# Every second softmax tile masked by ScalarE and GpSimd, with sb in three places

## The chip, the core and the metric

The kernel runs on one core of a Trainium2 chip. The metric is the device time of one execution in microseconds (us), the median of several runs. The engines are called PE (TensorE matmuls; PEld are its weight loads), DVE (VectorE), ACT (ScalarE), POOL (GpSimd) and SP (SyncE, which issues the DMAs).

## The reference

Attention in which each query keeps its 32 best scores, and behind it an expert layer with a product of two projections:

```
scores = scale * np.matmul(q, k.transpose(0, 1, 3, 2))      # q, k, v: (4, 8, 576, 64)
kth = np.partition(scores, -top_k, axis=-1)[..., -top_k:-top_k + 1]      # top_k = 32
scores = np.where(scores >= kth, scores, -1000000000.0)
scores = scores - np.max(scores, axis=-1, keepdims=True)
attn = np.exp(scores)
attn = attn / (np.sum(attn, axis=-1, keepdims=True) + 1e-09)
x = np.matmul(attn, v)                     # then as (2304 tokens, 512)
out = ((x @ w_a) * (x @ w_b)) @ w_out      # w_a, w_b: (512, 1536), w_out: (1536, 512)
```

## The kernel before

**Tiles and chunks.** The 2304 tokens are eight chunks: each of the four batches has one of 256 tokens and one of 320. Attention goes through 144 tiles in order. A tile is 64 queries of two heads against all 576 keys, so a matrix of 128 x 576; four tiles make a head pair of a chunk of 256 tokens, five one of 320. Tiles 0 to 15 are chunk 0, 16 to 35 chunk 1, 36 to 51 chunk 2, 52 to 71 chunk 3, and so on to 143.

**One tile.** `scores` has PE write the scores s to PSUM (L422; two places). `topk` has ScalarE copy them to sb in SBUF (two places), and VectorE finds the 32 largest in two columns' minima and maxima with MAX8 and MATCH_REPLACE8 (L442 to L452). The 32nd, `tb[:, g, 31:32]`, is the threshold. The tiles are taken in groups of two (GRP), so an even tile and the odd one behind it share the tiles mx and top, and behind the odd one GpSimd subtracts a 128x2 piece (L456, short). `softmax` then masks and exponentiates in one of two ways:
- P (the letter is that of the changed kernel): ScalarE makes r = relu(threshold - s) from PSUM (L470), PE subtracts a huge multiple of it from s by two bf16 matmuls with `nident` (L475), and ScalarE takes the exponential of s from PSUM with its sum (L477). s stays taken until then. Of the scores only half is copied to sb (L435).
- V: all of s is copied to sb (L433), ScalarE takes the exponential of sb (L464), and VectorE multiplies it by (sb >= threshold) and sums (L466).

Tiles 0 to 34 are P. From 35 to 109 the even ones are V and the odd ones P; from 110 on all are V. Behind either way come a small ScalarE step, VectorE's reciprocal (L480) and the scaling of p, by GpSimd (L484), or from tile 50 on by ScalarE in even tiles (L482). `transpose` turns p on PE (L497) and ScalarE copies it (L502). At the last tile of a head pair, `av` has PE multiply it with v (L525). When a chunk has all its pairs, its experts can run.

**Experts.** `up` makes a tile of the two projections from 12 matmuls each (L555 to L557, high and low parts), ScalarE or VectorE takes the product (L564, L569; L572 and L573 in the first two chunks), ScalarE writes gh and GpSimd the rest gl (L574, L575). `down` multiplies all of gh and gl with w_out (L585 to L587).

**What sets the order.** Nothing in the program runs in the order in which it is written. `Plan` lists all operations with an engine, a cost, a key and the buffers they need. It then goes through them with an event queue: an engine that is free takes the ready operation with the lowest key whose buffers have a place. Attention has keys from -1000 on, transpositions and weightings 0 to 143, experts 1000 and more, so experts fill what attention leaves of PE. Where PE has nothing to do and no product waits, Plan puts a filler matmul (L291, `mm<-still,nident`). The list that comes out is each engine's program, and each engine runs its own list strictly in order. In Plan's costs a masking pass of VectorE (`port=True`) takes 0.4 us longer when GpSimd is busy at its start.

```
plan.filler = (lambda: buf([128, 512], FT, "mm", 2, psum), FILL_N / 2353,
               lambda b: mm(b[:, 0:FILL_N], nident, still, start=True, stop=True))
ATTENTION, URGENT, EXPERTS = -1000, -1500, 1000
```

Of the kernel before, what the change touches and what calls it, by code (L numbers as in the profile page):

```python
# [8 lines left out]
FT = mybir.dt.float32  # L9
# [5 lines left out]
AF = mybir.ActivationFunctionType  # L15
OP = mybir.AluOpType
AX = mybir.AxisListType

HUGE = float(2.0 ** 94)
# [4 lines left out]
GRP = 2  # L24


VECTOR_MASK = (35, 110)
SCALAR_SCALE = 50
POOL_PRODUCT = 2
CONV_FIRST = 14  # L30
# [220 lines left out]
def attn_moe(ctx: ExitStack, tc, qT, kT, v, wa, wb, wo, out):  # L251
# [5 lines left out]
    nc = tc.nc  # L257
    B, NP, _, S = qT.shape
    NJ = wa.shape[0]
    HS = S // 2  # L260
# [18 lines left out]
        tiles += [dict(c=c, p=p, pair=c * NP + p, off=64 * s, s=s, n=n) for s in range(n // 64)]  # L279
    NT = len(tiles)  # L280

    def vector_mask(i):
        return i >= VECTOR_MASK[0] and i % 2 == 0 or i >= VECTOR_MASK[1]


    plan = Plan()
    key = [0.0]
    still = const.tile([128, FILL_N], BF, name="still")
# [4 lines left out]
    def buf(shape, dtype, tag, bufs, pool=work):  # L293
        return Buf(pool, shape, dtype, tag, bufs)

    def act(n, fn, r, w, ps=False, ptr=0, k=None):
        plan.op("ACT", n / 1200 + (0.085 if ps else 0.11) + 0.075 * ptr + 0.035 * (n == 1), key[0] if k is None else k, fn, r, w)

    def dve(n, fn, r, w, cost=None, k=None, port=False):
        plan.op("DVE", cost or (n + 76) / 960, key[0] if k is None else k, fn, r, w, port=port)  # L300

    def pool(n, fn, r, w, cost=None):
        plan.op("POOL", cost or 0.2 + n / 480, key[0], fn, r, w)

    def pe(cols, fn, r, w, rows=1.0, num=0, k=None):
        plan.op("PE", cols / 2300 + 0.009 * num, key[0] if k is None else k, fn, r, w, rows=rows)
# [119 lines left out]
    def topk(i, s):  # L426

        alone = vector_mask(i)  # L430
        sb = buf([128, 2, HS], FT, "sb", 2)
        if alone:
            act(S, lambda: nc.scalar.activation(sb.ap, s[:, :, 0:HS], AF.Copy), [s], [sb], ps=True)  # L433
        else:
            act(HS, lambda: nc.scalar.activation(sb[:, 1], s[:, 1, 0:HS], AF.Copy), [s], [sb], ps=True)  # L435
        g = i % GRP
        if g == 0:
            tops.append((buf([128, GRP, HS + 8], FT, "mx", 2), buf([128, GRP, 32], FT, "top", 2)))
        mx, tb = tops[-1]
        mn, t8, bias = buf([128, HS], FT, "mn", 1), buf([128, 8], FT, "t8", 2), buf([128, 1], FT, "bias", 3)  # L440

        dve(HS, lambda: vec.tensor_tensor(mn.ap, s[:, 0, 0:HS], sb[:, 1], OP.min), [s, sb], [mn])  # L442
        dve(HS, lambda: vec.max(mx[:, g, HS:HS + 8], mn.ap), [mn], [(mx, g, 1)])
        dve(HS, lambda: vec.tensor_tensor(mx[:, g, 0:HS], s[:, 0, 0:HS], sb[:, 1], OP.max), [s, sb], [(mx, g, 0)])
        tk = [t8] + [(tb, g, r) for r in range(1, 4)]

        def eight(r):
            return tb[:, g, 8 * r:8 * r + 8] if r else t8.ap
        for r in range(4):
            dve(HS + 8, lambda r=r: vec.max(eight(r), mx[:, g]), [(mx, g, 0), (mx, g, 1)], [tk[r]], 0.393)  # L450
            if r < 3:
                dve(HS + 8, lambda r=r: vec.match_replace(mx[:, g], eight(r), mx[:, g], LOW), [tk[r]], [(mx, g, 0), (mx, g, 1)], 0.453)  # L452
            if r == 0:
                act(1, lambda: nc.scalar.activation(bias.ap, t8[:, 0:1], AF.Copy, scale=-0.125), [t8], [bias], k=URGENT)
        if g == GRP - 1:
            pool(g, lambda: nc.gpsimd.tensor_tensor(short[:, i - g:i + 1], tb[:, :, 31], mx[:, :, HS + 7], OP.subtract),  # L456
                 [(mx, x, y) for x in range(GRP) for y in (0, 1)] + [(tb, x, 3) for x in range(GRP)], [("short", i)])
        return bias, (tb, g, tk[3]), sb

    def softmax(i, s, found):  # L460
        bias, (tb, g, tok), sb = found
        pt, sm = buf([128, 2, HS], FT, "p", 3), buf([128, 2], FT, "sm", 3)
        if vector_mask(i):
            act(S, lambda: nc.scalar.activation(pt.ap, sb.ap, AF.Exp, bias=bias.ap, scale=0.125),  # L464
                [sb, bias], [pt], ptr=1)
            dve(S, lambda: vec.scalar_tensor_tensor(pt.ap, sb.ap, tb[:, g, 31:32], pt.ap, op0=OP.is_ge, op1=OP.mult,  # L466
                                                    accum_out=sm[:, 0:1]), [sb, tok], [pt, sm], 0.735, port=True)
        else:
            r = buf([128, 2, HS], BF, "r", 2)
            act(S, lambda: nc.scalar.activation(r.ap, s[:, :, 0:HS], AF.Relu, bias=tb[:, g, 31:32], scale=-1.0),  # L470
                [s, tok], [r], ps=True, ptr=1)

            def mask():
                for g in range(2):
                    mm(s[:, g, 0:HS], nident, r[:, g], start=False, stop=True, skip_group_check=True)  # L475
            pe(S, mask, [r], [s])
            act(S, lambda: nc.scalar.activation(pt.ap, s[:, :, 0:HS], AF.Exp, bias=bias.ap, scale=0.125,  # L477
                                                accum_out=sm[:, 0:1]), [s, bias], [pt, sm], ps=True, ptr=2)
        act(1, lambda: nc.scalar.activation(sm[:, 1:2], sm[:, 0:1], AF.Copy, bias=1e-9), [], [sm], k=URGENT)
        dve(1, lambda: vec.reciprocal(sm[:, 1:2], sm[:, 1:2]), [], [sm])  # L480
        if i >= SCALAR_SCALE and i % 2 == 0:
            act(S, lambda: nc.scalar.activation(pt.ap, pt.ap, AF.Copy, scale=sm[:, 1:2]), [sm], [pt], ptr=1)  # L482
        else:
            pool(0, lambda: nc.gpsimd.tensor_scalar(pt.ap, pt.ap, sm[:, 1:2], 1.0, op0=OP.mult, op1=OP.mult), [sm], [pt], 0.81)  # L484
        return pt
# [113 lines left out]
    for i, t in enumerate(tiles):  # L599
        c, pi = t["c"], t["pair"]  # L600
        key[0] = ATTENTION + i
        s = scores(i)
        pt = softmax(i, s, topk(i, s))
        key[0] = i + TURN
        transpose(i, pt)
# [177 lines left out]
```

## Time and profile before

| | |
|---|---|
| median of 3 runs | 899.75 us (899.21 to 903.09) |
| the profiled execution | 903.89 us, of which the span is 902.2 us |
| mean granted TensorE clock in its span | 0.982 |
| busy: PE, PEld, DVE | 834.0 (92%), 663.4 (74%), 747.3 us (83%) |
| busy: ACT, POOL | 566.8 (63%), 321.3 us (36%) |
| chain of work that ended last, by engine | PE 73%, DVE 11%, ACT 5%, POOL 3%, DMA 3% |

An engine's busy time is the union of its instructions' times. Matmuls overlap in a pipeline and their ends are modelled, so what one costs is read from the starts of those around it.

### The profile page before, as it was taken

To read this page: it belongs to the slowest core of one execution; us is meant where nothing else is said; L and a number is where in the kernel's file an instruction comes from. 1 tells how busy PE (TensorE), PEld (TensorE's weight loads), DVE (VectorE), ACT (ScalarE), POOL (GpSimd) and SP (SyncE) were. 2 spreads that over 40 slices of the span, in tenths; PEclk is the share of its full clock that TensorE was granted. 3 is DMA by queue.
4 is the path that set the end of the run, shared out by engine and by line. 5 is a ranking of instruction groups with operands and counts; after the bars stand their busy time and mean duration, and the time that the engine had idled before them with its cause. 6 is when DMAs were issued, how large, how long until landed. Compare 5 with 4: busy or idle time off the path is not lost.

```text
span 902.2 us, 18725 instructions
## 1 busy us (share of the span) xinstructions
PE 834.0 (92%) x6461; PEld 663.4 (74%) x6461; DVE 747.3 (83%) x2310; ACT 566.8 (63%) x1334; POOL 321.3 (36%) x431
## 2 busy tenths in 40 slices
PE   3767779997999999999999999999999999999997
PEld 1433347765768867887787888787878888899997
DVE  4899888999999999999999999999999999960010
ACT  3678667995767776777666676677666665651120
POOL 2677655885335541232213231122212221331120
PEclk8999999998999999999999999999999999999999
DMA  5767754874336741476226662377326732475450
GB/s 192 235 220 237 233 177 154 313 249 149 106 112 210 221 138 57 125 252 228 87 68 217 207 202 80 103 241 240 116 81 213 245 117 77 139 232 172 141 208 28
DMA packets 75430, 153.87 MB, mean 171 GB/s; under 512 B 7232, under 2 KB 46144, under 8 KB 75328
## 3 DMA queue, kind: packets, MB, share of 16 engines
q1 hardware_dynamic: 75328, 152.60, 52.6%
q8 instruction: 53, 0.87, 0.4%
q14 instruction: 49, 0.40, 0.2%
HBM read 135.27 MB, written 17.30 MB: 169 GB/s over the span
## 4 chain that ended last, share of the span: by engine, by line
PE 73%; DVE 11%; ACT 5%; POOL 3%; DMA 3%; issue 3%; SPq 1%; POOLq 0%; ACTq 0%; DVEq 0%
PE mm L555 11%; PE mm L557 10%; PE mm L556 10%; PE s L422 8%; PE tp L497 7%; PE mm L525 7%; PE mm L585 6%; PE mm L587 5%; PE mm L586 5%; DVE mx L452 3%; DVE top L450 2%; PE s L475 2%; DMA wo<-wb 1%; POOL wo L389 1%; DMA gh<-wb 1%
## 5 line engine op out<-in xcount | busy, mean ns | idle before, releaser
L555 PE MATMUL mm<-xh,w 128*128 128x256 f32 (+1 forms) x768 | 241.9, 315 | 1.8 <-DMA w<-wd 1.7
L557 PE MATMUL mm<-xh,w 128*128 128x256 f32 (+1 forms) x768 | 226.8, 295 | 0.0
L556 PE MATMUL mm<-xl,w 128*128 128x256 f32 (+1 forms) x768 | 226.5, 295 | 0.0
L450 DVE MAX8 top<-mx 128x8 f32<-128x296 f32 x432 | 196.1, 459 | 2.9
L555 PEld LDWEIGHTS mm<-xh,w 128*128 128x128 f32 x768 | 144.6, 188 | 30.6 <-issue 27.0
L556 PEld LDWEIGHTS mm<-xl,w 128*128 128x128 f32 x768 | 144.9, 189 | 0.0
L557 PEld LDWEIGHTS mm<-xh,w 128*128 128x128 f32 x768 | 144.2, 188 | 0.0
L502 ACT ACTIVATE pt<-tp 128x640 f32<-128x640 f32 x144 | 101.2, 703 | 66.8 <-PE tp L497 66.2
L575 POOL TENSOR_TENSOR gl<-a,gh 128x256 fp32r<-128x256 f32 (+1 forms) x96 | 78.4, 817 | 175.2 <-ACT gh L574 172.9
L452 DVE MATCH_REPLACE8 mx<-top,mx 128x296 f32<-128x296 f32 x288 | 129.9, 451 | 0.0
L422 PE MATMUL s<-kr,qr 64*64 64x288 f32 x1152 | 107.3, 442 | 17.8 <-ACT p L477 10.7
L585 PE MATMUL mm<-gh,wo 128*128 128x256 f32 (+1 forms) x384 | 122.0, 318 | 0.3 <-ACT b L591 0.2
L484 POOL TENSOR_SCALAR p<-p,sm 128x576 f32<-128x576 f32 x97 | 81.1, 836 | 111.6 <-DVE sm L480 104.4
L497 PE MATMUL tp<-ident,p 128*128 128x128 f32 x720 | 104.8, 276 | 12.7 <-POOL p L484 11.6
L586 PE MATMUL mm<-gl,wo 128*128 128x256 f32 (+1 forms) x384 | 114.2, 297 | 0.4 <-POOL gl L575 0.4
L587 PE MATMUL mm<-gh,wo 128*128 128x256 f32 (+1 forms) x384 | 114.4, 298 | 0.1
L497 PEld LDWEIGHTS tp<-ident,p 128*128 128x128 f32 x720 | 82.7, 141 | 28.8 <-POOL p L484 20.5
L569 DVE SCALAR_TENSOR_TENSOR a<-mm,a 128x256 f32<-128x256 f32 (+1 forms) x72 | 32.8, 455 | 79.2 <-PE mm L557 76.3
L585 PEld LDWEIGHTS mm<-gh,wo 128*128 128x128 f32 x384 | 73.3, 191 | 16.6 <-issue 13.6
L525 PE MATMUL mm<-pt,vr 128*64 128x256 f32 (+1 forms) x640 | 84.7, 411 | 0.8 <-ACT pt L502 0.6
L442 DVE TENSOR_TENSOR mn<-s,sb 128x288 f32<-128x288 f32 x144 | 64.4, 447 | 18.8 <-ACT sb L435 17.7
L586 PEld LDWEIGHTS mm<-gl,wo 128*128 128x128 f32 x384 | 73.4, 191 | 0.6 <-POOL gl L575 0.6
(82 smaller groups left out, 1459.2 us busy)
## 6 DMA issues: line engine op xcount, KB each, us to landing
w<-wd SPq DMA_DIRECT2D x168, 512.0 KB, 4.4
wd<-w SPq DMA_DIRECT2D x24, 512.0 KB, 3.4
kr<-kT SPq DMA_DIRECT2D x64, 144.0 KB, 3.0
vr<-v SPq DMA_DIRECT2D x32, 256.0 KB, 2.9
wo<-wa SPq DMA_DIRECT2D x12, 512.0 KB, 5.2
qr<-qT SPq DMA_DIRECT2D x32, 160.0 KB, 3.2
wo<-wb SPq DMA_DIRECT2D x9, 512.0 KB, 5.7
qr<-qT SPq DMA_DIRECT2D x32, 128.0 KB, 3.0
```

What stands on the lines that cost most here:

```text
L422: mm(s[rows, g, 0:HS], qr[on, h, t["off"]:t["off"] + 64], kr[on, h, :], start=True, stop=True)
L450: dve(HS + 8, lambda r=r: vec.max(eight(r), mx[:, g]), [(mx, g, 0), (mx, g, 1)], [tk[r]], 0.393)
L452: dve(HS + 8, lambda r=r: vec.match_replace(mx[:, g], eight(r), mx[:, g], LOW), [tk[r]], [(mx, g, 0), (mx, g, 1)], 0.453)
L497: nc.tensor.transpose(tp[:, kb, :], pf[:, k0:k0 + 128], ident)
L502: act(640, lambda: nc.scalar.activation(turned[:, :, :, t["off"]:t["off"] + 64], tp.ap.rearrange("p k (h q) -> p k h q", h=2), AF.Copy), [ ...
L525: mm(ps[e, :n], vr[:, kb, e], turned[:, kb, h, :n], start=(kb == 0), stop=(kb == 4))
L555: mm(ps[:, :n], w[:, 0, kb, :], xh[:, kb, :n], start=(kb == 0), stop=False)
L556: mm(ps[:, :n], w[:, 0, kb, :], xl[:, kb, :n], start=False, stop=False)
L557: mm(ps[:, :n], w[:, 1, kb, :], xh[:, kb, :n], start=False, stop=(kb == 3))
L585: mm(ps[:, :n], fin[j][:, 0, ms], gh[:, j, :n], start=(j == 0), stop=False)
L586: mm(ps[:, :n], fin[j][:, 0, ms], gl[:, j, :n], start=False, stop=False)
L587: mm(ps[:, :n], fin[j][:, 1, ms], gh[:, j, :n], start=False, stop=(j == NJ - 1))
```

## The change

The pair of numbers that told V tiles apart becomes a string with a letter for each tile. Tiles 0 to 34 stay P, even tiles from 36 on are V as before, and all odd tiles from 35 on become Q: the 38 from 35 to 109 were P, the 17 from 111 to 143 were V. No tile from 35 on is masked through PE. In a Q tile GpSimd makes threshold x HUGE (far), ScalarE makes relu(far - HUGE x sb) from the copy in SBUF, GpSimd subtracts that from sb (576 columns, two inputs), and ScalarE takes the exponential with its sum. All of s is copied to sb for Q as for V, and sb has three places for two.

```diff
-VECTOR_MASK = (35, 110)
+MASKS = "P" * 35 + "QV" * 55
...
-    def vector_mask(i):
-        return i >= VECTOR_MASK[0] and i % 2 == 0 or i >= VECTOR_MASK[1]
...
-        alone = vector_mask(i)
-        sb = buf([128, 2, HS], FT, "sb", 2)
-        if alone:
+        sb = buf([128, 2, HS], FT, "sb", 3)
+        if MASKS[i] != "P":
             act(S, lambda: nc.scalar.activation(sb.ap, s[:, :, 0:HS], AF.Copy), [s], [sb], ps=True)
...
-        if vector_mask(i):
+        if MASKS[i] == "Q":
+            far = buf([128, 1], FT, "far", 2)
+            pool(1, lambda: nc.gpsimd.tensor_scalar(far.ap, tb[:, g, 31:32], HUGE, None, op0=OP.mult), [tok], [far])
+            act(S, lambda: nc.scalar.activation(pt.ap, sb.ap, AF.Relu, bias=far.ap, scale=-HUGE), [sb, far], [pt], ptr=1)
+            pool(S, lambda: nc.gpsimd.tensor_tensor(pt.ap, sb.ap, pt.ap, OP.subtract), [sb], [pt])
+            act(S, lambda: nc.scalar.activation(pt.ap, pt.ap, AF.Exp, bias=bias.ap, scale=0.125, accum_out=sm[:, 0:1]),
+                [bias], [pt, sm], ptr=2)
+        elif MASKS[i] == "V":
```

Plan makes a new order from this. Up to the end of chunk 0's experts the lists are the same. In the changed kernel line numbers are 4 or 5 lower up to `topk`, and 2 higher from `softmax`'s V branch on.

PE around the weighting of tile 71 (pt and vr), the last of chunk 3, before. Ahead of it end the up products of chunk 2 (xh, xl), behind it begin its down products (gh, gl):

```order
L557 MATMUL mm<-xh,w 128x256
L497 MATMUL tp<-ident,p 128x128 x5
L291 LDWEIGHTS nident
L291 MATMUL mm<-still,nident 128x256
...
L525 MATMUL mm<-pt,vr 64x320 x10
L497 MATMUL tp<-ident,p 128x128 x5
L422 MATMUL s<-kr,qr 64x288 x4
L475 LDWEIGHTS nident
L475 MATMUL s<-r,nident 128x288
...
L585 MATMUL mm<-gh,wo 128x256
```

The same place now:

```order
L499 MATMUL tp<-ident,p 128x128 x5
L557 MATMUL mm<-xh,w 128x256
L558 MATMUL mm<-xl,w 128x256
L559 MATMUL mm<-xh,w 128x256
L527 MATMUL mm<-pt,vr 64x320 x10
L418 MATMUL s<-kr,qr 64x288 x4
L499 MATMUL tp<-ident,p 128x128 x5
L587 MATMUL mm<-gh,wo 128x256
```

Four fillers (one of them is shown) and a mask's two matmuls are gone, and up products stand right ahead of the weighting, where before there were fillers. Of the other fillers from 250 us on, the 9 ahead of tile 35's weighting have become 19, and 7 around the end of chunk 1's up products have become 2.

DVE in chunk 3, where the last two tiles (70 is V, 71 is Q) and the first two of chunk 4 meet, before. top_5831 belongs to tiles 70 and 71, top_6014 to the next two; L466 is the masking pass of a V tile, L450 into top a step of the search, L480 the reciprocal:

```order
L466 SCALAR_TENSOR_TENSOR p_5843,sm_5877<-sb_5750,top_5831,p_5843 128x576
...
L450 MAX t8_5983<-mx_5957 128x8
L450 MAX top_5831<-mx_5782 128x8
L452 MATCH_REPLACE mx_5957<-t8_5983,mx_5957 128x296
...
L480 RECIPROCAL sm_6022<-sm_6022 128x1
```

The same place now; here top_5858 belongs to tiles 70 and 71, and sm_6033 is tile 71's:

```order
L468 SCALAR_TENSOR_TENSOR p_5845,sm_5932<-sb_5709,top_5858,p_5845 128x576
L447 MATCH_REPLACE mx_5791<-top_5858,mx_5791 128x296
...
L445 MAX top_5858<-mx_5791 128x8
L438 MAX mx_5974<-mn_5953 128x8
...
L482 RECIPROCAL sm_6033<-sm_6033 128x1
L445 MAX top_6024<-mx_5974 128x8 x2
L447 MATCH_REPLACE mx_5974<-top_6024,mx_5974 128x296 x2
L445 MAX top_6024<-mx_5974 128x8 x2
L468 SCALAR_TENSOR_TENSOR p_6019,sm_6096<-sb_5876,top_6024,p_6019 128x576
```

Between tile 71's last MAX and its reciprocal stand 8 vector operations before and 12 now (among them three replacements), and 19 now between that MAX and the next masking pass (among them five replacements).

POOL in the same stretch, before (gl is the experts', short the 128x2 piece of a pair, L484 the scaling):

```order
L575 TENSOR_TENSOR gl_5254<-a_5857,gh_5250 128x256
L575 TENSOR_TENSOR gl_5254<-a_5912,gh_5250 128x256
L456 TENSOR_TENSOR short_99<-top_5831,mx_5782 128x2
L575 TENSOR_TENSOR gl_5254<-a_5970,gh_5250 128x256
L484 TENSOR_SCALAR p_6021<-p_6021,sm_6022 128x576
```

Now:

```order
L577 TENSOR_TENSOR gl_5289<-a_5888,gh_5283 128x256
L451 TENSOR_TENSOR short_99<-top_5858,mx_5791 128x2
L460 TENSOR_SCALAR far_5984<-top_5858 128x1
L577 TENSOR_TENSOR gl_5289<-a_5928,gh_5283 128x256
L462 TENSOR_TENSOR p_5993<-sb_5772,p_5993 128x576
L577 TENSOR_TENSOR gl_5289<-a_5986,gh_5283 128x256
L486 TENSOR_SCALAR p_5993<-p_5993,sm_6033 128x576
```

The product far and the subtraction of tile 71 (p_5993) have come between the short piece and the scaling, each next to an expert's gl. In 39 of the 55 Q tiles nothing stands between far and the subtraction; in 4 the memset of vr (L336 now) does, which waits for PE.

## Rows read from the trace of the kernel before

**Rows 1.** Busy by stage: window, length, PE, PEld, DVE, ACT, POOL, clock, DMA.
```profile
250.00:434.00 184.00, 180.01 (x1435) 142.44 (x1433) 173.84 (x573) 130.25 (x319) 64.39 (x96) 1.00 0.54 170
434.00:625.00 191.00, 189.71 (x1520) 152.36 (x1521) 179.57 (x595) 132.09 (x317) 46.44 (x78) 1.00 0.50 156
625.00:802.00 177.00, 176.61 (x1367) 148.56 (x1367) 169.71 (x547) 110.64 (x246) 41.97 (x68) 1.00 0.49 155
802.00:902.20 100.20, 93.77 (x716) 91.28 (x715) 8.10 (x20) 18.85 (x45) 15.08 (x20) 0.99 0.43 144
```

**Rows 2.** What PE waited for, 250 to 802 us: total, times, longest.
```profile
PE tp L497 <- POOL p L484: 3.5, 5, 1.1
PE s L475 <- ACT r L470: 1.1, 2, 0.8
PE s L422 <- ACT p L477: 0.5, 2, 0.3
```

**Rows 3.** The mask's matmuls on PE (L475) in a window, columns as in rows 1.
```profile
250.00:625.00 375.00, 15.85 (x76) 1.00 0.52 162
```

**Rows 4.** Timeline of PE: a mask between two experts (start, duration).
```profile
329.52 0.31 PE L557 MATMUL mm<-xh,w 128*128 128x320 f32 x1
329.67 0.42 PE L475 MATMUL s<-r,nident 128*128 128x288 bf16 x2
329.83 0.40 PE L555 MATMUL mm<-xh,w 128*128 128x320 f32 x1
330.07 0.30 PE L556 MATMUL mm<-xl,w 128*128 128x320 f32 x1
```

**Rows 5.** Timeline of PE: a mask behind a transposition.
```profile
458.75 0.41 PE L475 MATMUL s<-r,nident 128*128 128x288 bf16 x2
458.90 0.37 PE L585 MATMUL mm<-gh,wo 128*128 128x256 f32 x1
```

**Rows 6.** Timeline of PE around 332 us.
```profile
331.98 0.93 PE L291 MATMUL mm<-still,nident 128*128 128x256 bf16 x5
334.03 0.76 PE L497 MATMUL tp<-ident,p 128*128 128x128 f32 x5 [1.11 <-POOL p L484]
...
334.96 0.41 PE L585 MATMUL mm<-gh,wo 128*128 128x320 f32 x1
```

**Rows 7.** Timeline around 433 us: PE, and a masking pass of DVE.
```profile
432.79 0.80 PE L291 MATMUL mm<-still,nident 128*128 128x256 bf16 x4
...
433.60 1.21 DVE L466 SCALAR_TENSOR_TENSOR p<-sb,top,p 128x576 f32<-128x576 f32 x1
434.03 2.91 PE L525 MATMUL mm<-pt,vr 128*64 128x320 f32 x20 [0.45 <-ACT pt L502]
```

**Rows 8.** Groups by shape on POOL, 250 to 802 us: busy, mean ns, idle before.
```profile
L484 POOL TENSOR_SCALAR p<-p,sm 128x576 f32<-128x576 f32 x62 | 50.8, 820 | 89.9 <-DVE sm L480 82.9 <-PE s L422 4.2 <-DVE short L651 1.5
L575 POOL TENSOR_TENSOR gl<-a,gh 128x320 fp32r<-128x320 f32 x42 | 37.6, 896 | 68.3 <-ACT gh L574 68.3
L575 POOL TENSOR_TENSOR gl<-a,gh 128x256 fp32r<-128x256 f32 x24 | 17.8, 743 | 43.9 <-ACT gh L574 41.6 <-ACT sm L479 2.3
...
L456 POOL TENSOR_TENSOR short<-top,mx 128x2 f32<-128x2 f32 x54 | 11.6, 215 | 105.1 <-DVE top L450 103.3 <-DMA w<-wd 1.5
```

**Rows 9.** Groups by shape on ACT, 250 to 802 us.
```profile
L464 ACT ACTIVATE p<-sb,bias 128x576 f32<-128x576 f32 x71 | 54.8, 772 | 1.3
L433 ACT ACTIVATE sb<-s 128x576 f32<-128x576 f32 x70 | 45.0, 643 | 4.7 <-PE s L422 2.2 <-DVE sm L480 1.6 <-DVE mx L444 0.5
...
L470 ACT ACTIVATE r<-s,top 128x576 bf16<-128x576 f32 x38 | 28.0, 737 | 7.9 <-DVE top L450 7.6
...
L435 ACT ACTIVATE sb<-s 128x288 f32<-128x288 f32 x37 | 15.1, 407 | 6.4 <-PE s L422 5.6 <-PE s L475 0.7
```

**Rows 10.** The masking pass: durations in ns (least/median/most), and its group by shape.
```profile
L466 DVE SCALAR_TENSOR_TENSOR p<-sb,top,p x71: 797/814/1518, 255.4 to 799.9; 128x576 f32<-128x576 f32 x71
...
L466 DVE SCALAR_TENSOR_TENSOR p<-sb,top,p 128x576 f32<-128x576 f32 x71 | 64.1, 903 | 1.7 <-ACT p L464 1.5 <-ACT bias L454 0.2
```

## The prediction

> **What bounds the kernel now.** I read the busy time by stage first. From 250 us on PE is the engine that never rests: 180.01 of 184.00 us, 189.71 of 191.00, 176.61 of 177.00, and then a tail of 100 us in which VectorE has nothing left (8.10 us) and PE works through the experts that remain [rows 1]. PE's granted clock is 1.00 in these stages, which is the 2.4 GHz level. VectorE is nearly as full (173.84 of 184.00), but it ends 100 us before the kernel does. So VectorE decides when attention ends, and PE decides when the kernel ends. Next I read what PE waits for between 250 and 802 us: 3.5 us for softmax tiles that GpSimd scales, 1.1 us for the relu and 0.5 us for the exponential of P tiles [rows 2]. That is 5.1 us of 552. A microsecond of PE work saved here is therefore nearly a microsecond saved at the end, and a microsecond of new waiting is one lost: PE's order is fixed when the program is built, so it can't do another expert when a transposition is late.
>
> **What is removed from PE.** 38 tiles (35, 37, ... 109) change from P to Q and lose two 288-column matmuls each: 76 between 250 and 625 us [rows 3]. What one pair costs is read from the starts, since the ends overlap. Between two experts, the matmul of L557 starts at 329.52, the mask at 329.67, the next expert at 329.83, and the one after it only at 330.07 [rows 4]. At the pitch of 0.15 us that the first two show, that last one would have started at 329.82: the pair costs 0.25 us, since the first expert behind it is held up too. In the order 19 pairs stand so. The other 19 stand beside a score, a transposition or a weighting of v, where such a hold-up is paid anyway; there I count only from the mask's start to that of the next matmul, 458.75 to 458.90, 0.15 us [rows 5]. Sum: 19 x 0.25 + 19 x 0.15 = **7.6 us less**. Bounds: 38 x 0.15 = 5.7 and 38 x 0.25 = 9.5.
>
> **Where PE runs dry.** At three places PE idles or runs filler matmuls. The order shows them as fillers: 9 before tile 35's weighting, 7 around 332 us, 4 before tile 71's; in the changed order they are 19, 2 and 0. At 332 us PE has five fillers and a wait from 331.98 to 334.03, then a transposition, then two more until 334.96: 2.98 us less the 0.76 in which the transposition is busy, 2.2 us [rows 6]. At 433 us it is 434.03 - 432.79 = 1.2 us [rows 7]. If the new order holds on the chip, up to 3.1 us come back (two fillers stay, some 0.3); if not, none. I take **2.0 less**. At tile 35 it goes the other way. Its chain now has the threshold product, like the 128x2 subtraction of 0.215 us, and the big subtraction. That one is not in the trace. The nearest rows are GpSimd's 128x256 and 128x320 subtractions, 0.743 and 0.896 us, so 2.39 ns a column and 0.743 + 320 x 2.39 ns = 1.51 us for 576 columns [rows 8]. Its lower bound is the one-input pass over 576 columns, 0.820 us [rows 8], its upper one 1.51 and a wait for the masking pass, 2.3; two inputs speak for 1.51. So 1.7 us join the chain, and the mask's 0.42 us leave it [rows 4, 8]: the weighting of tile 35's pair starts up to 1.3 us later. But two scores more are done before it, work that is not owed later. I take **0.5 more** (0 to 1.3).
>
> **What is added elsewhere, and what hides it.** ScalarE: a full copy for a half one, 0.643 for 0.407 us, and relu and exponential from SBUF at 0.772 instead of 0.737 from PSUM [rows 9]: 0.31 us x 38 = 12 us into stages in which ScalarE idles 113 of 375 us [rows 1]. In the 17 tiles from 111 on, which were V, a relu comes on top, 0.77 us or about 1 us with the read of its sum, 17 us into 66 idle. These 17 tiles give VectorE back its masking pass, 17 x 0.81 = 14 us [rows 10]. That hides behind PE, which is full there; were PE idle, it would be worth up to those 14. GpSimd: 55 x (1.51 + 0.2) = 94 us, and it is idle 399 of 552 us [rows 1]. Third place for sb and the earlier release of s let ScalarE copy and PE score ahead; they cost PE nothing, and the 0.5 us of waits of scores for an exponential fall away, as do the 1.1 for the relu [rows 2].
>
> Behind each GpSimd subtraction ScalarE's queue holds the exponential, and behind that copies that free PSUM; VectorE's queue holds a reciprocal. In the order 12 vector operations stand between tile 71's last maximum and its reciprocal. At 0.30 us for an instruction (173.84 / 573 [rows 1]) and with the load that each of three replacements brings, that is 4.5 us, against a chain of 0.2 + 0.2 + 0.77 + 1.51 + 0.77 + 0.2 and six hand-overs that I put at 0.1 each, 4.3 us. It fits, but barely; a few will be late. I take 0.05 us for each of 55 tiles, 2.8, less the 1.6 of P's waits: **1.2 more** (-1.6 to +8).
>
> The port is the other risk. The row: VectorE's masking pass lasts 0.814 us at the median, 0.903 in the mean, 1.518 at most [rows 10]; so 71 x 0.089 = 6.3 us are already lost, while GpSimd was busy 28% of the time [rows 1]. One stands at 433.60 with 1.21 us [rows 7]. The Trainium skill ("SBUF — State Buffer", section "SBUF: two separate sides") says that VectorE with two SBUF inputs and GpSimd lock a shared pair of ports, and the one that comes second blocks for the whole instruction. By that rule a pass of a V tile that meets a subtraction would wait up to its 1.5 us; the stretched rows agree with it. By the order they seldom meet: between a pair's last maximum, which starts the subtraction's chain, and the next masking pass stand 19 vector operations, 24 with the loads, some 7 us, and the subtraction is done after 2.8. The sum without the rule is the one below; if the passes do meet it, the time is the second rival's.
>
> **Sum.** -7.6 - 2.0 + 0.5 + 1.2 = -7.9, and I round to -7.5 for lateness that I can't see. The profiled execution took 903.89 us (span 902.2), 4.1 above the median of 899.75, so 896.4 for it and **892.2 us** as the median.
>
> **The rivals.**
> *Late in order (20%).* Each Q tile's probability arrives 0.15 us late and PE waits: 55 x 0.15 = 8 us instead of 2.8, and the dry places stay: about -7.6 + 0.5 + 6.6 = -0.5, 899. For it: 4 of the 55 subtractions stand behind the memset of vr, which waits for PE. Against it: V tiles, whose chain hangs on three engines too, cost PE almost nothing between 625 and 802 us (0.4 us idle) [rows 1].
> *The port decides; slower (10%).* If each of the 37 V tiles before 625 us waits half a subtraction, 0.75 us, VectorE loses 28 us, some 25 more than now. It idles 21.6 us there [rows 1]; with half of that usable, attention falls some 14 us behind the order and PE with it: -7.5 + 14 = +6.5, 906. The point from which it decides is 0.58 us for each tile ((7.5 + 10.8 + 3.3) / 37, where 3.3 is 37 x 0.089).
> *The masks were free (8%).* If PE's time is not the bound before 434 us, only the 19 later masks count: -3.8 + 0.5 + 1.2 = about -2, 897.5. PE idles 4.0 of 184 us there [rows 1], which speaks against it.
> *All of it (7%).* -9.5 - 3.1 + 0.5, and new waits no longer than the old: about -12, 888.
>
> **How the numbers follow.** The forecast has 55%, with 890 to 896. This kernel can be told from no change at 0.5%, 4.5 us: faster is below 895.25. Nine tenths of the forecast, all of the last rival and a little of the others lie there: 0.59. Within 0.5%: the two rivals near 898 and the forecast's rest, 0.31. Slower: the port, 0.10. The range from 887 to 899.5 leaves out the port's case and half of "late in order".
>
> **What the new profile would show.** No matmul into s from nident after tile 34; PE still above 97% busy from 260 us to the end; fillers near 250 us with tile 35's weighting about a microsecond later in its run of work, and none near 430. GpSimd's 576-column subtraction at 1.5 us; the masking pass at a mean of 0.9 us or below. Attention on VectorE ends clearly before 800 us and PE's tail is longer. I am wrong if PE's waits for the scaled tiles grow from 3.5 us to 8 and more, if the masking pass goes to 1.2 us in the mean, or if PE's clock falls near 250 us, where it now idles longer.

## The result, and the profile after

The changed kernel takes **884.88 us** (median of 4 runs, 881.12 to 888.2) against 899.48 (median of 4, 897.24 to 903.09): a ratio of 0.984, with a 95% interval of 0.9805 to 0.9876. It is 14.6 us faster. The prediction had 7.5 us and a range that ended at 887.0. The profiled execution took 888.20 us (span 886.5), 15.7 less than that of before.

Busy time by stage of the changed kernel, columns as in rows 1, the last two stages moved forward by some 15 us:

```profile
250.00:434.00 184.00, 181.52 (x1459) 144.47 (x1458) 176.25 (x600) 138.48 (x332) 95.62 (x140) 1.00 0.55 174
434.00:625.00 191.00, 191.00 (x1547) 158.71 (x1546) 181.81 (x608) 138.50 (x324) 76.25 (x119) 1.00 0.54 169
625.00:787.00 162.00, 161.63 (x1247) 133.72 (x1246) 139.75 (x473) 112.41 (x259) 63.75 (x96) 1.00 0.46 143
787.00:886.00 99.00, 93.19 (x708) 91.90 (x706) 8.05 (x18) 17.81 (x43) 14.06 (x18) 1.00 0.44 153
```

PE is as full as before, 191.00 of 191.00 us in the second stage. Where VectorE stops is not seen from the last window: its last reciprocal starts at 775.0 us, for 801.2 before, and PE's last matmul at 880.76, for 896.34. PE's tail without VectorE is thus 106 us for 95, longer as the prediction said. So it is still PE that ends last, with less to do. What PE waited for while attention ran (total, times, longest) went from 5.5 us, the 5.1 of [rows 2] and this line,

```profile
PE mm L525 <- ACT pt L502: 0.4, 1, 0.4
```

to 2.6 between 250 and 787 us:

```profile
PE tp L499 <- POOL p L486: 1.5, 2, 0.9
PE mm L527 <- ACT pt L504: 0.7, 2, 0.4
PE mm L557 <- DVE one L657: 0.4, 1, 0.4
```

The new operations, as groups by line between 250 and 787 us (busy, mean ns, idle time before):

```profile
L462 POOL TENSOR_TENSOR p<-sb,p 128x576 f32<-128x576 f32 x55 | 78.1, 1420 | 43.4 <-ACT p L461 23.9 <-ACT bias L449 19.2 <-DMA w<-wd 0.3
L460 POOL TENSOR_SCALAR far<-top 128x1 f32<-128x1 f32 x55 | 11.8, 214 | 0.0
L461 ACT ACTIVATE p<-sb,far 128x576 f32<-128x576 f32 x55 | 42.6, 774 | 10.6 <-POOL far L460 10.1
L463 ACT ACTIVATE p<-p,bias 128x576 f32<-128x576 f32 x55 | 42.3, 769 | 4.1 <-POOL p L462 3.6
```

The subtraction takes 1.42 us (1.51 was worked out) and the threshold product 0.21 (0.2).

**Where PE's time went.** Ends overlap, so I add up the distances from each matmul's start to the next one's, by kind, from the weighting of tile 35's pair (it starts at 255.35 us before, 257.47 after) to the last matmul (896.34 before, 880.76 after):

| kind of matmul, start to next start, us | before | after | difference |
|---|---|---|---|
| masks (74 of 76 are recorded before, none after) | 6.9 | 0 | -6.9 |
| experts, the same 3,024 in both | 441.2 | 433.6 | -7.7 |
| fillers | 4.8 | 1.7 | -3.1 |
| scores (one tile fewer is left to do) | 68.4 | 66.8 | -1.6 |
| transpositions | 54.9 | 56.5 | +1.6 |
| weightings | 64.7 | 64.7 | 0.0 |
| sum | 641.0 | 623.3 | -17.7 |

The stretch starts 2.1 us later, so the last matmul comes 15.6 us earlier. The masks' row is near what the prediction had. Of the experts' 7.7 us, 1.9 are the masks' as well: 20 of the 37 recorded pairs stood between two experts and held up the expert behind them by 0.09 us each, which is in the prediction's 0.25. Another 1.3 us are waits of PE that stand behind an expert. The other 4.5 us are the line that the prediction lacks: the same products cost less because they are cut less often. Two places in the order on PE after, first a score behind a weighting, then one behind a transposition (start, duration):

```profile
400.72 2.91 PE L527 MATMUL mm<-pt,vr 128*64 128x320 f32 x20
403.56 0.72 PE L418 MATMUL s<-kr,qr 64*64 64x288 f32 x8
404.21 0.39 PE L557 MATMUL mm<-xh,w 128*128 128x256 f32 x1
404.44 0.28 PE L558 MATMUL mm<-xl,w 128*128 128x256 f32 x1
404.55 0.28 PE L559 MATMUL mm<-xh,w 128*128 128x256 f32 x1
...
409.17 0.71 PE L499 MATMUL tp<-ident,p 128*128 128x128 f32 x5
409.81 0.72 PE L418 MATMUL s<-kr,qr 64*64 64x288 f32 x8
410.45 0.39 PE L557 MATMUL mm<-xh,w 128*128 128x256 f32 x1
...
411.39 0.28 PE L558 MATMUL mm<-xl,w 128*128 128x256 f32 x1
411.51 0.28 PE L559 MATMUL mm<-xh,w 128*128 128x256 f32 x1
411.71 0.72 PE L418 MATMUL s<-kr,qr 64*64 64x288 f32 x8
```

The first expert behind other work takes 0.23 us to the next start (404.21 to 404.44), the second 0.11: each time a run of experts is entered again, about 0.1 us is lost, as behind the mask of [rows 4]. The last expert ahead of a score loses nearly as much (411.51 to 411.71, where 411.39 to 411.51 is the pace). When a score stands behind a weighting or a transposition, the loss of entering is paid once for both. From the ninth weighting (tile 39's pair) on, runs of experts were cut 190 times before, 74 of them by scores and 18 by masks; after it is 147, and 51 by scores.

### The profile page after: what moved, and what is told of

It is laid out like the page before. It is cut to its first block, busy times and chain, and to the rows that moved or that the text cites. A ratio compares the mean times of both kernels' runs of the same rounds, so it can differ in the third digit from the quotient of the medians.

```text
span 886.5 us, 18664 instructions
## 1 busy us (share of the span) xinstructions
PE 825.2 (93%) x6386; PEld 660.1 (74%) x6386; DVE 723.1 (82%) x2276; ACT 582.2 (66%) x1368; POOL 403.1 (45%) x541
## 4 chain that ended last, share of the span: by engine, by line
PE 73%; DVE 10%; ACT 5%; POOL 4%; issue 3%; DMA 2%; SPq 1%; POOLq 0%; ACTq 0%; DVEq 0%
PE mm L557 11%; PE mm L559 10%; PE mm L558 10%; PE s L418 8%; PE tp L499 8%; PE mm L527 7%; PE mm L587 6%; PE mm L589 6%; PE mm L588 6%; DVE mx L447 2%; DVE top L445 2%; DVE wo L388 1%; POOL wo L385 1%; POOL p L486 1%; DVE wo L386 1%
## 5 line engine op out<-in xcount | busy, mean ns | idle before, releaser
L445 DVE MAX8 top<-mx 128x8 f32<-128x296 f32 x432 | 190.4, 457 | 1.4
L486 POOL TENSOR_SCALAR p<-p,sm 128x576 f32<-128x576 f32 x97 | 77.9, 803 | 99.1 <-DVE sm L482 99.0
L418 PE MATMUL s<-kr,qr 64*64 64x288 f32 x1152 | 106.3, 441 | 16.9 <-ACT p L479 10.1
L499 PE MATMUL tp<-ident,p 128*128 128x128 f32 x720 | 107.3, 281 | 10.2 <-POOL p L486 9.5
L462 POOL TENSOR_TENSOR p<-sb,p 128x576 f32<-128x576 f32 x55 | 78.1, 1420 | 43.4 <-ACT p L461 23.9
L576 ACT ACTIVATE gh<-a 128x256 fp32r<-128x256 f32 (+1 forms) x96 | 42.4, 441 | 57.5 <-DVE a L571 54.2
```

Of the source, the lines that this page charges most:

```text
L418: mm(s[rows, g, 0:HS], qr[on, h, t["off"]:t["off"] + 64], kr[on, h, :], start=True, stop=True)
L499: nc.tensor.transpose(tp[:, kb, :], pf[:, k0:k0 + 128], ident)
```

## The experiments

All are held against the kernel before on the same chip (897.9 to 899.5 us). Two figures are read from each profiled execution besides the time. **Lead**: from the first score product of a tile (L418) to the end of VectorE's maximum over its keys (L439), the mean of tiles 37 to 109; it says how far PE scores ahead of VectorE. **Length**: from the ninth weighting's start to the last matmul. It leaves out the first 270 us, in which one execution differs from another (the ninth weighting starts between 269.6 and 280.0 us, in no order that follows the edits).

| kernel | median, us | ratio (95%) | lead, us | cuts (by scores) | length, us |
|---|---|---|---|---|---|
| before | 897.9 to 899.5 | 1 | 4.44 | 190 (74) | 618.7 |
| changed | 884.88 | 0.984 (0.9805 to 0.9876) | 8.57 | 147 (51) | 605.7 |
| e1 third place of sb alone | 899.17 | 1.0018 (0.9989 to 1.0046) | 4.52 | 177 (70) | 619.1 |
| e2 the 38 P tiles alone | 882.99 | 0.9844 (0.9804 to 0.9884) | 8.57 | 152 (59) | 605.7 |
| e3 the 17 V tiles alone | 898.94 | 1.0016 (0.9989 to 1.0043) | 4.52 | 177 (73) | 619.0 |
| e4 two places of sb | 960.36 | 1.0706 (1.067 to 1.0743) | 10.96 | 102 (57) | 674.0 |
| e5 idle products in the scores | 893.72 | 0.9924 (0.9896 to 0.9952) | 8.45 | 142 (60) | 610.7 |
| e6 idle products at the masks | 895.32 | 0.9974 (0.9949 to 0.9999) | 5.17 | 144 (60) | 612.2 |
| e7 s held | 893.04 | 0.993 (0.9903 to 0.9958) | 4.29 | 166 (72) | 612.2 |
| e9 tile 35 stays P | 886.94 | 0.9853 (0.9817 to 0.9888) | 8.50 | 140 (54) | 603.5 |
| e10 four places of sb | 884.3 | 0.9839 (0.9811 to 0.9866) | 8.52 | 153 (58) | 606.7 |
| e11 relu from tile 15 | 900.76 | 1.0014 (0.9985 to 1.0043) | 8.78 | 144 (56) | 619.5 |
| e12 idle products and s held | 896.92 | 0.9985 (0.9965 to 1.0005) | 4.07 | 170 (63) | 616.1 |
| e13 two relu tiles in three | 888.93 | 0.9896 (0.9863 to 0.993) | 8.49 | 158 (78) | 607.4 |

Gains are compared by the ratios; the difference of two of them has, worked out from theirs, an interval of some 0.0045, or 4 us, to each side. Lead, cuts and length come from one execution of each kernel. And every edit makes Plan build a new order: e2, e10 and e13 leave PE's work and the release of s in the 38 tiles as they are in the changed kernel, and their medians still lie between 883.0 and 888.9 us. So a part of a few microseconds can be the new order alone, which was not separated.

My first theory was PE's time: the masks, the cuts around them, and scores that stand better because s comes free earlier. The rivals were VectorE's relief in 17 tiles and the third place of sb by itself.

### Which part of the change: e1, e2, e3, e4

**e1**, the kernel before with

```diff
-        sb = buf([128, 2, HS], FT, "sb", 2)
+        sb = buf([128, 2, HS], FT, "sb", 3)
```

> The kernel before with sb in 3 places and nothing else. Theory PE time (the gain of 14.6 us is TensorE time: 38 masks of about 0.25 us, the interruptions of expert runs that go with them, and scores that stand in better places because s comes free earlier): the masks are still on PE and s is still held to the exponential, so within 0.3% of before, 897 to 902 us. Theory places (the third place of sb alone lets the scores run ahead): most of the gain is here, 885 to 892 us.

899.17 us, no change, and a lead of 4.52 us as before. Places alone give nothing.

**e2**, the changed kernel with only the P tiles changed:

```diff
-MASKS = "P" * 35 + "QV" * 55
+MASKS = "P" * 35 + "QV" * 37 + "Q" + "V" * 34
```

> Only the 38 tiles that TensorE masked (35 to 109, odd) go to the relu and the subtraction; the 17 odd tiles behind 110 stay on VectorE. sb in 3 places. Theory PE time: 38 masks and their interruptions are gone, so 10 to 15 us of the gain is here, 884.5 to 890 us. Theory VectorE (the gain beyond the masks' 7.6 us is the 17 passes of 0.9 us that VectorE loses late in the program): only the masks' 7 to 8 us, 891 to 893 us.

882.99 us: all of the gain.

**e3**, with only the late V tiles changed:

```diff
-MASKS = "P" * 35 + "QV" * 55
+MASKS = "P" * 35 + "PV" * 37 + "P" + "VQ" * 17
```

> Only the 17 odd tiles behind 110 go from VectorE to the relu and the subtraction; the 38 masks stay on TensorE. sb in 3 places. Theory PE time: TensorE's work is that of before, so 898 to 901 us. Theory VectorE: 5 to 8 us of the gain is here, 891 to 895 us.

898.94 us, nothing. The theory of VectorE's relief falls: its 14 us hide behind a full PE.

**e4**, the changed kernel with sb in two places:

```diff
-        sb = buf([128, 2, HS], FT, "sb", 3)
+        sb = buf([128, 2, HS], FT, "sb", 2)
```

> The changed kernel with sb in 2 places again. Theory PE time in its plain form: TensorE's work is the same, and s comes free at the copy either way, so within 2 us of the changed kernel, 883 to 887 us. If the earlier scores need a free place of sb as well (the relu and the subtraction hold it longer than the mask on TensorE did), the part of the gain that goes beyond the masks is lost, and the time is 888 to 893 us. Theory places: all of the gain is lost, 895 us or more.

960.36 us, 75 more than the changed kernel. "895 us or more" allows it, but no theory had a reason for this size. What PE waited for between 250 and 887 us in e4, and its fillers in all from 250 us on (duration in ns, first and last start):

```profile
PE s L418 <- ACT p L484: 15.3, 7, 3.3
PE s L418 <- DVE sm L482: 4.6, 2, 2.5
PE s L418 <- DVE mx L439: 3.2, 6, 1.3
...
L287 PE MATMUL mm<-still,nident x214: 269/270/421, 250.0 to 930.6; 128*128 128x256 bf16 x107
```

214 fillers stand there, for 25 in the changed kernel: PE ran out of work that was ready. One such place, all engines, only the steps of scores, sb and the masking:

```profile
439.21 0.72 PE L418 MATMUL s<-kr,qr 64*64 64x288 f32 x8
...
439.86 5.62 PE L287 MATMUL mm<-still,nident 128*128 128x256 bf16 x34
444.34 1.40 POOL L462 TENSOR_TENSOR p<-sb,p 128x576 f32<-128x576 f32 x1 [0.89 <-ACT p L461]
445.77 0.78 ACT L463 ACTIVATE p<-p,bias 128x576 f32<-128x576 f32 x1 [0.85 <-POOL p L462]
...
446.54 0.63 ACT L428 ACTIVATE sb<-s 128x576 f32<-128x576 f32 x1
447.20 0.46 DVE L437 TENSOR_TENSOR mn<-s,sb 128x288 f32<-128x288 f32 x1 [0.85 <-ACT sb L428]
```

Scores are written at 437.48 and 439.21, and both places of s are full; the next copy starts at 446.54, when the subtraction of an earlier tile has given a place of sb back and the exponential ahead of the copy is through. PE runs fillers for 5.6 us, and VectorE has its next minimum only at 447.20, after 0.85 us idle. On average a relu tile keeps sb for 10.7 us in e4 (from the copy's start to the subtraction's end; 13.9 us in the changed kernel, where it need not hurry), a VectorE tile 10.6. With two places that allows a tile every 5.3 us at best; the copies of tiles 37 to 109 came every 5.88 us in e4, and every 4.77 in the changed kernel. The third place is worth nothing alone and is the condition of the rest.

### Which part of PE's side: e5, e6, e7, e12

**e5** adds work that computes nothing: products of a zero tile into s, in the block of the scores of the 38 tiles.

```diff
...
+            if 35 <= i < 110 and i % 2:
+                for g in range(2):
+                    mm(s[:, g, 0:HS], nident, zero, start=False, stop=True, skip_group_check=True)
...
```

> The changed kernel, with TensorE time put back where it interrupts nothing: in the 38 tiles that TensorE masked before (35 to 109, odd) the scores are followed, in the same block, by two products of a zero tile of 288 columns that add nothing to them. 76 products of 0.125 us are 9.5 us of TensorE. Theory PE time in its plain form (TensorE's own time is all there is): 9 to 10 us of the gain goes, 893 to 895 us. Theory interruptions (about half of the gain is that expert runs are cut less often and the scores stand better, and that stays here): also 893 to 895, but then the run with the same products at the masks' places must be some 4 to 6 us longer than this one. Theory release (the gain is s coming free earlier, not TensorE's time): 885 to 888 us.

893.72 us; the difference of the ratios to the changed kernel, 0.0084, is 7.5 us. In its trace, counted as in the table above, the zero products take 7.0 us and the experts 433.8, as in the changed kernel (433.6). PE's time for the masks, without any place in the order, is half of the gain.

**e6** puts the same products behind the threshold, as an entry of its own:

```diff
...
+            def idle():
+                for h in range(2):
+                    mm(s[:, h, 0:HS], nident, zero, start=False, stop=True, skip_group_check=True)
+            if i < 110:
+                pe(S, idle, [tok], [s])
```

> The changed kernel, with the same 76 zero products where the masks stood: an entry of TensorE's of its own behind the threshold, which cuts an expert's run and keeps s until then. The softmax itself stays with ScalarE's relu and GpSimd's subtraction. Theory PE time in its plain form: as the run with the products among the scores, 893 to 895 us. Theory interruptions: all of the gain is lost, 897 to 901 us. Theory release: as far as s is kept to the threshold and not to the exponential, half of the gain, 890 to 893 us.

895.32 us, 0.0134 or 12 us. That is 0.005 (4.5 us) more than e5 by the ratios, a little beyond what the two intervals leave (some 0.004), but only 1.6 us more by the medians. Its profiled execution, 889.17 us, was its fastest of 12. In the order that came out the products cut an experts' run only 6 times, where the masks did so 18 times, and the entry also keeps s to the threshold: the lead falls to 5.17 us. So the pair does not say what the masks' places in the order cost.

**e7** adds no work; s only counts as taken until the exponential:

```diff
             act(S, lambda: nc.scalar.activation(pt.ap, pt.ap, AF.Exp, ...),
-                [bias], [pt, sm], ptr=2)
+                [bias, s], [pt, sm], ptr=2)
```

> The changed kernel with s kept, in the order's rules, to the exponential of the relu tiles (as the kernel before kept it in the tiles that TensorE masked, but here some 3 us longer, behind the relu and the subtraction); no work is added. Theory PE time in its plain form: within 2 us of the changed kernel, 883 to 887 us. Theory interruptions (the scores stand better because s comes free at the copy): 4 to 6 us longer, 888 to 892 us. Theory release: all of the gain goes, 897 us or more.

893.04 us: 0.009 or 8 us go without a single instruction more, between what two of the theories said. From the first score product to the exponential s is kept 14.5 us on average in the odd tiles 37 to 109, and 13.3 in these tiles before, when they were P; in the changed kernel it goes at VectorE's maximum, after 8.5. The lead falls to 4.29 us, the scores cut experts 72 times again (74 before), and PE's waits between 250 and 787 us come back:

```profile
PE tp L499 <- POOL p L486: 5.0, 8, 1.4
PE mm L527 <- ACT pt L504: 0.8, 1, 0.8
```

Counted as in the table above, the experts take 439.5 us (433.6 in the changed kernel) and the fillers 6.0 (1.7). The edit holds s in all 55 relu tiles, though in the 17 from 111 on the kernel before had let it go at VectorE's maximum. These 17 cost little: fillers and what the experts take beyond their steady pace (0.12 us for 256 columns, 0.147 for 320) come to 25.4 us in e7 and 15.5 in the changed kernel up to the first score of tile 111, and to 9.8 and 9.5 behind it.

My theory was too narrow: it took PE's time for the main thing and s for a help; as far as the intervals tell, they are worth the same.

**e12** is e6 with s also kept to the exponential:

```diff
-                [bias], [pt, sm], ptr=2)
+                [bias, *[s] * (i < 110)], [pt, sm], ptr=2)
```

> The run with 76 zero products where the masks stood, and s kept to the exponential in those 38 tiles as well: all that the change took from TensorE's side is put back, while ScalarE and GpSimd still do the masking. If TensorE's side (masks, cuts of the experts, s) is the whole gain: 897 to 903 us, as the kernel before. If something else has a part in it (the 17 tiles that VectorE lost, the third place): 893 us or less.

896.92 us, 0.9985 (0.9965 to 1.0005): with both put back the kernel before is reached to within 0.35%, though the relu, the subtraction, the third place and VectorE's 17 passes are as in the changed kernel. PE's side is the gain, but for at most the 3 us that the interval leaves, and it has two parts. The parts are not restored in the same shape: the experts take 436.0 us here, 441.2 before. The zero products between 250 and 802 us (duration in ns, first and last start), all 76 recorded:

```profile
L463 PE MATMUL s<-zero,nident x76: 286/286/299, 251.5 to 626.3; 128*128 128x288 bf16 x76
```

### What binds next: e9, e10, e11, e13

**e9** leaves tile 35 as it was:

```diff
-MASKS = "P" * 35 + "QV" * 55
+MASKS = "P" * 36 + "VQ" * 54
```

> Tile 35 stays with TensorE, and from 36 on VectorE and the relu take turns as in the changed kernel; this undoes the change at its first tile alone, where the weighting of tile 35 began 2.2 us later than before. Theory boundary (those 2.2 us are lost for good): 882 to 883.5 us. Rival (the lateness is made up behind it): as the changed kernel, 884 to 886 us.

886.94 us: no gain that shows, though the interval reaches down to 883 us. In its trace the weighting of tile 35's pair starts at 252.5 us, 5 us before that of the changed kernel, and the ninth weighting at 275.3, for 275.1: the lateness at tile 35 is made up behind it.

**e10** gives sb a fourth place:

```diff
-        sb = buf([128, 2, HS], FT, "sb", 3)
+        sb = buf([128, 2, HS], FT, "sb", 4)
```

> The changed kernel with sb in 4 places. In the changed kernel's trace a relu tile keeps its place of sb for 13.9 us on average from the copy's start to the subtraction's end, and a VectorE tile 12.8 us; three places then allow a tile every 4.3 to 4.6 us, close to the pace that TensorE keeps (about 4.7 us a tile). Theory TensorE's pace (the places no longer bind once there are three): within 2 us of the changed kernel, 883 to 887 us. Theory places still bind: 876 to 882 us.

884.3 us, as the changed kernel (the lead is 8.52): three places are enough for PE's pace.

**e11** begins with the relu at tile 15, among P tiles:

```diff
-MASKS = "P" * 35 + "QV" * 55
+MASKS = "P" * 15 + "QP" * 10 + "QV" * 55
```

> The changed kernel with the relu also in every second tile of 15 to 33, where TensorE masked; ten more masks and ten more holds of s go. Theory TensorE's pace (each tile that leaves TensorE gives back 0.2 to 0.4 us: 14.6 us for 38 tiles): 2 to 4 us off, 881 to 883 us. Rival VectorE's pace (in the first 250 us TensorE is busy for 198 us of 250 and VectorE for 217, so TensorE's time is not what counts there): within 1 us of the changed kernel, 884 to 886 us, or longer by what the relu adds to a tile's chain (about 2.2 us at tile 35), 887 us.

900.76 us: the whole gain is lost, more than the rival's bound. Busy time between 220 and 300 us in e11 (columns as in rows 1):

```profile
220.00:260.00 40.00, 27.39 (x197) 18.98 (x195) 39.21 (x124) 26.75 (x61) 24.63 (x31) 0.82 0.32 100
260.00:300.00 40.00, 37.23 (x298) 25.91 (x297) 38.70 (x134) 26.27 (x66) 19.87 (x30) 0.93 0.39 117
```

and in the changed kernel:

```profile
220.00:260.00 40.00, 35.25 (x268) 24.98 (x267) 35.06 (x111) 25.85 (x63) 13.77 (x21) 0.91 0.31 102
260.00:300.00 40.00, 39.10 (x316) 31.15 (x313) 38.51 (x134) 30.54 (x77) 26.28 (x37) 1.00 0.62 197
```

VectorE is full in both windows, and PE is busy 9.7 us less of 80, at a granted clock of 0.82 and 0.93. There PE waits 5.9 us for scores whose place VectorE's maximum still holds, and 5.1 us for tiles that GpSimd scales. Attention ends earlier (VectorE's last search step starts at 752 us, for 769), but from 434 us on PE is full and can't make the loss up. Why the order leaves this hole isn't settled.

**e13** uses the relu in two tiles of three:

```diff
-MASKS = "P" * 35 + "QV" * 55
+MASKS = "P" * 35 + "QQV" * 37
```

> From tile 35 on two tiles in three are masked by the relu and the subtraction and one by VectorE: 18 more passes of 0.9 us leave VectorE, and 18 more relus of 0.77 us and subtractions of 1.42 us go to ScalarE and GpSimd. Theory TensorE's pace: no work of TensorE changes, 883 to 887 us. Theory VectorE: 875 to 881 us. Theory places (a relu tile keeps sb 1.1 us longer than a VectorE tile): 887 to 892 us.

888.93 us. Still more relief for VectorE gives nothing, which agrees with e3. That it is some 4 us longer than the changed kernel fits the rule of the places, but its interval (0.9863 to 0.993) reaches into the changed kernel's, and its lead (8.49) shows no shortage; open. No variant beats the changed kernel by more than the noise.

## Why the prediction was wrong

The direction and the bound were right: PE decides, and what leaves it comes off the end. The size was half. None of the signs by which the prediction would have known itself wrong came (waits for the scaled tiles of 1.5 us, a masking pass of 0.897, a granted clock of 1.00 from 240 to 280 us), since all of them looked for a loss. Point by point:

- **Masks, -7.6.** Right within its bounds: 6.9 us from start to start for the 74 that are recorded, 8.8 with the 1.9 by which 20 pairs held up the expert behind them, and 7.5 us when e5 puts products of the same size back.
- **Dry places, -2.0.** Right in kind, nearer its bound: the fillers came out as the order had them (19, 2 and 0 at the three places) and give 3.1 us back.
- **Tile 35, +0.5.** Mis-sized and without effect. Its weighting started 2.1 us later, beyond the bound of 1.3; after the fillers its transposition waited for GpSimd's scaling:

```profile
252.89 2.35 PE L287 MATMUL mm<-still,nident 128*128 128x256 bf16 x14
255.91 0.77 PE L499 MATMUL tp<-ident,p 128*128 128x128 f32 x5 [0.67 <-POOL p L486]
256.51 0.71 PE L287 MATMUL mm<-still,nident 128*128 128x256 bf16 x4
257.47 2.91 PE L527 MATMUL mm<-pt,vr 128*64 128x320 f32 x20 [0.25 <-ACT pt L504]
```

  But e9, without that, is no faster.
- **New waits, +1.2.** Wrong in sign: PE's waits fell from 5.5 to 2.6 us, 1.6 of it at the two dry places (the 1.11 of [rows 6] and the 0.45 of [rows 7]) and so 1.3 besides, near the lower bound of -1.6. With s held in e7 they are 5.8 us, but 2.2 in e12, which holds it too, and 4.2 in e10, which does not; what sets them is not shown.
- **"Third place for sb and the earlier release of s let ScalarE copy and PE score ahead; they cost PE nothing."** This is the step that failed. I booked it at nothing, as a cost that is absent, and didn't ask what it brings. e7 measures the release of s at 8 us, give or take 4: the lead doubles, scores cut the experts' runs 51 instead of 74 times, and PE waits less. It needs the third place (e4), which alone does nothing (e1). I had priced how a mask delays the expert behind it, and not asked how the scores, moved by the same change, stand among the experts.
- **VectorE's 14 us hide behind PE.** Right (e3, e13).
- **Rivals.** *Late in order* didn't come: waits fell. *The port decides* didn't either: none of the 54 masking passes overlaps a 576-column subtraction, as the distances in the order said; their mean is 0.897 us for 0.903 in [rows 10]. *The masks were free* left the masks 3.8 us; e5 takes back 7.5, though its interval just reaches 3.8. *All of it* was nearest, and still 3 us short, since it had no term for the release of s.

What stays open is why the order puts scores with a longer lead beside other work more often; this wasn't tried, and the lead alone doesn't decide it: in e13 it is 8.49 us and scores cut the runs 78 times, in e6 5.17 us and 60 times. How the 8 us of e7 divide is read from single traces only (5.9 us of experts, with the waits behind them, and 4.3 us of fillers).

## What to carry to other kernels

When an edit frees a buffer earlier, ask who is waiting for that place and where in the bottleneck engine's order the work will now stand: here that was worth about as much as the work removed. A chain that keeps a buffer longer needs places for its whole life divided by the pace (13.9 us at 4.77 us a tile is 2.9, so three), and one place fewer cost 75 us where the extra place alone gave nothing. To split a gain, put the removed time back as idle work and the removed hold back as a dependency, each alone and then both.

## What the runs showed of the hardware

Masking passes on VectorE are stretched by ordinary GpSimd passes. All 12 of the 54 that took over 0.85 us overlap one; the longest (start, duration):

```profile
473.18 0.88 POOL L577 TENSOR_TENSOR gl<-a,gh 128x320 fp32r<-128x320 f32 x1 [1.89 <-ACT gh L576]
473.25 1.42 DVE L468 SCALAR_TENSOR_TENSOR p<-sb,top,p 128x576 f32<-128x576 f32 x1
```

GpSimd started 0.07 us earlier, and the pass took 0.62 us longer than the median of 0.80. In all 12 GpSimd had started first, by 0.07 to 0.50 us, and the pass ended 0.60 to 0.62 us after GpSimd did. Another 22 passes overlap a GpSimd instruction of over 0.4 us and were not stretched: in 14 of them a GpSimd instruction that had started earlier ended within 0.21 us of the pass's start, and in 8 VectorE was first. There GpSimd's instruction is the longer one, the more so the sooner it follows, up to this one of 1.42 us, where 14 of the 16 of its line and size take 0.87 to 0.89:

```profile
679.60 0.81 DVE L468 SCALAR_TENSOR_TENSOR p<-sb,top,p 128x576 f32<-128x576 f32 x1
679.73 1.42 POOL L531 TENSOR_TENSOR xl<-xf,xh 128x320 fp32r<-128x320 f32 x1 [0.80 <-ACT xh L530]
```

The Trainium skill ("SBUF — State Buffer", section "SBUF: two separate sides") says that whichever of the two starts first gets the shared ports for the whole instruction and the other waits; the trace agrees in both directions, with the 0.62 us above for VectorE and 0.55 us here for GpSimd.

GpSimd's subtraction with two inputs of 576 columns was steady, 1.408 to 1.443 us in all 55; the 1.51 that I drew from narrower subtractions was 0.09 us too long. The Trainium skill ("GPSIMD Engine Reference", section "3.1 Elementwise — side-by-side cycle accounting") has 4497 ns for 2048 columns, which by proportion is an estimate of 1.26 us; the trace is 0.16 us above it.
